# Loading v for batches two to four with casting transfers from GpSimd's queue

## The chip, the cores and the metric

The kernel runs on one core of a Trainium2 chip. The core has a TensorE (PE in the profile), a VectorE (DVE), a ScalarE (ACT), a GpSimd (POOL) and a SyncE (SP), each of which works through its own instructions in their order, and 16 DMA engines that they share. The time is the device time of one execution in microseconds; three runs of the kernel before gave 247.18, 247.3 and 246.52, median 247.18 us.

## What is computed

A retention layer feeds a Fourier mixing block with an MLP. There are 4 batches, 8 heads, 768 steps and 64 elements per head:

```python
for t in range(S):
    state = gamma[None, :, None, None] * state + np.einsum('bhd,bhe->bhde', k[:, :, t], v[:, :, t])
    y[:, :, t] = scale * np.einsum('bhd,bhde->bhe', q[:, :, t], state)

x = attn_out.transpose(0, 2, 1, 3).reshape(B, S, H * D)
mixed = np.real(np.fft.fft(np.fft.fft(x, axis=1), axis=2))
u = x + mixed
un = (u - mu) / np.sqrt(var + 1e-06)        # layer norm over the 512 features
out = u + np.maximum(un @ w_ch1, 0.0) @ w_ch2
```

The inputs q, k, v and the two weight matrices (512x2048 and 2048x512) are float32; the output is float32, 4 x 768 x 512.

## The kernel before

**Retention in chunks.** The 768 steps are cut into 6 chunks of 128, which lie on the 128 partitions, and heads are taken in pairs, so a batch has four steps of one head pair each. For a pair, q, k and v arrive as float32 tiles of 128 partitions x 768 elements. GpSimd makes 16-bit tiles of them: `q16`, `kd` (k times a decay per row) and `v16`. TensorE then forms the products of queries and keys inside each chunk (`a_unit`, line 600; VectorE masks them into `atm`, line 603), the state contribution of each chunk (`kv_unit`, line 619, a matmul of `kd` and `v16`; VectorE chains them into `s16`, line 629), and the output (`y_unit`: line 650 multiplies q by the states, line 654 multiplies `atm` by `v16`). In the first two batches TensorE transposes q and k (lines 439 and 556); in the last two the DMA engines do, in transfers that SP issues (lines 548 and 550).

**The mixing and the MLP.** The Fourier transforms are matmuls with tables (lines 736 and 833), with symmetric halves folded by VectorE (lines 679 to 705). GpSimd adds x to the result u (lines 870 and 872), VectorE takes the statistics, ScalarE subtracts the mean (line 891). The MLP runs in two halves of 384 rows per batch: `h_unit` (line 936, lines 953 for the first rows) and `ch_unit` (line 979), whose output VectorE scales and adds to u and SP stores (line 987).

**The order of the work.** Tiles come from pools of fixed size: 11 float32 input tiles for q, k and v, 4 for `v16`, 3 for `kd`. The first batch's retention is written out by hand in `first_units`, in a fixed order for every engine. Behind it, streams of units are merged by times of their own: the MLP of batch b, the retention of batch b + 1 (`attn_steps`) and its mixing. A step of `attn_steps` emits the casts of pair i (`cast_unit`), the state products of pair i - 1 (`kv_unit`) and the output of pair i - 2 (`y_unit`). A unit wrapped in `held` follows on each engine behind the instruction that was emitted last. A wait in front of an instruction therefore holds up everything that is behind it on its engine.

**The loads.** All of q, k and v are issued by SP at line 165, three transfers of 384 KB per pair, in runs of 256 bytes (q of the first two batches in runs of 1536 bytes). The loads of the second batch wait for the seventh of the eight weight transfers and for a matmul of the first batch's MLP; those of the third and fourth wait for a score matmul of the batch before. The eight weight transfers (lines 993 and 1000) are issued by GpSimd, since they turn float32 into 16-bit on the way; each reads 1 MB in runs of 2 KB and writes 512 KB.

**The cast of v.** In `cast_unit` the cast of v (line 388) is the last of a pair's casts on GpSimd, behind q (line 373, or 380) and the two halves of kd (line 383). It reads the float32 tile with the head outside the chunk and writes `v16` with the chunk outside the head:

```python
v16 = vp.tile([P, NCH, 2, D], f16, tag="v16", name="v16")
last_cast[b, i] = nc.gpsimd.tensor_scalar(
    out=v16, in0=v32.rearrange("p h c d -> p c h d"), scalar1=1.0, scalar2=1.0,
    op0=ALU.mult, op1=ALU.mult)
```

In the first batch `v0_unit` does this (line 423), for the last pair half on VectorE (line 427).

Of the kernel before, what the change touches and what calls it, by code (L numbers as in the profile page):

```python
# [12 lines left out]
ALU = mybir.AluOpType  # L13
f32 = mybir.dt.float32
f16 = mybir.dt.float16
# [3 lines left out]
P = 128  # L19
# [24 lines left out]
def kernel(  # L44
# [106 lines left out]
                nc.tensor.matmul(wps, wz[:, 0:P], wz, start=True, stop=True)  # L151
        return run

    in_of, a_of = {}, {}
    w_dma = []
    srcs = {"q": q, "k": k, "v": v}

    def load_unit(b, i, after=None):
        def run():
            h0 = 2 * PAIR_ORDER[i]  # L160
            for name, src in srcs.items():
                t = inp.tile([P, 2, NCH, D], f32, tag="in32", name=f"{name}32")
                rows = "h (p c) d -> p h c d" if b < NPE and name == "q" else \
                    "h (c p) d -> p h c d"
                dma = nc.sync.dma_start(t, src[b, h0:h0 + 2].rearrange(rows, p=P))  # L165
                if after is not None:
                    for x in (w_dma[after].ins, lb[0]["mm"].ins):
                        tc.add_manual_dep(dma.ins, x.name,
                                          mybir.DependencyInfo(mybir.DependencyClass.Sync,
                                                               mybir.DependencyReason.DATA),  # L170
                                          reason="loads in turn")
                if b > 1:
                    tc.add_manual_dep(dma.ins, a_of[b - 1, 1].ins.name,
                                      mybir.DependencyInfo(mybir.DependencyClass.Sync,
                                                           mybir.DependencyReason.DATA),
                                      reason="loads behind the transposes")
                in_of[name, b, i] = t
        return run

    for i in range(4):  # L180
        load_unit(0, i)()
# [174 lines left out]
    x_edges(0)()  # L356


    at, q16_of, kd_of, v16_of, last_cast = {}, {}, {}, {}, {}

    def cast_unit(b, i):
        def run():
            h0 = 2 * PAIR_ORDER[i]
            q32, k32, v32 = (in_of.pop((n, b, i)) for n in "qkv")
            kd = kp.tile([P, NCH, 2, D], f16, tag="kd16", name="kd16")
            v16 = vp.tile([P, NCH, 2, D], f16, tag="v16", name="v16")
            with ExitStack() as es:
                if b < NPE:
                    if (b, i - 1) in last_cast:
                        es.enter_context(tc.issue_after(last_cast[b, i - 1].ins))  # L370
                    q16 = qzs[i % 2].rearrange("p h c d -> p (h c d)")[
                        :, 0:NCH * P].rearrange("p (c h d) -> p c h d", c=NCH, h=2)
                    es.enter_context(tc.issue_after(nc.gpsimd.tensor_scalar(
                        out=q16, in0=q32.rearrange("p h c d -> p c h d"), scalar1=1.0,
                        scalar2=1.0, op0=ALU.mult, op1=ALU.mult).ins))
                else:
                    q16 = qzs[i % 2]
                    for h2 in range(2):
                        dst = q16[:, h2, :, D * h2:D * h2 + D]
                        nc.gpsimd.tensor_scalar(out=dst, in0=q32[:, h2], scalar1=1.0,  # L380
                                                scalar2=1.0, op0=ALU.mult, op1=ALU.mult)
                for h2 in range(2):
                    kc = nc.gpsimd.tensor_scalar(out=kd[:, :, h2, :], in0=k32[:, h2],  # L383
                                                 scalar1=gkd[:, h0 + h2:h0 + h2 + 1],
                                                 scalar2=1.0, op0=ALU.mult, op1=ALU.mult)
                    if b < NPE:
                        es.enter_context(tc.issue_after(kc.ins))
                last_cast[b, i] = nc.gpsimd.tensor_scalar(  # L388
                    out=v16, in0=v32.rearrange("p h c d -> p c h d"), scalar1=1.0, scalar2=1.0,
                    op0=ALU.mult, op1=ALU.mult)  # L390
            q16_of[b, i], kd_of[b, i], v16_of[b, i] = q16, kd, v16
        return run

    def q0_unit(i):
# [22 lines left out]

    def v0_unit(i):
        def run():
            v32 = in_of.pop(("v", 0, i)).rearrange("p h c d -> p c h d")  # L420
            v16 = v16_of[0, i] = vp.tile([P, NCH, 2, D], f16, tag="v16", name="v16")
            n = NCH if i < 3 else 3
            last_cast[0, i] = nc.gpsimd.tensor_scalar(
                out=v16[:, 0:n], in0=v32[:, 0:n], scalar1=1.0, scalar2=1.0, op0=ALU.mult,
                op1=ALU.mult)
            if n < NCH:
                nc.vector.tensor_copy(v16[:, n:], v32[:, n:])
        return run

    def t0_unit(i, part):  # L430
# [46 lines left out]
    def kv0_unit(i):  # L477
        def run():
            st = at[0, i]
            kd, v16 = kd_of[0, i], v16_of[0, i]  # L480
            wkf = st["wkf"] = ps_g.tile([P, D * (NCH - 1)], f32, tag="g", name="wkK",
                                        padded_shape=[P, DM])
            wk = wkf.rearrange("p (e c) -> p e c", c=NCH - 1)
            for c in range(NCH - 1):
                for h2 in range(2):
                    nc.tensor.matmul(wk[64 * h2:64 * h2 + 64, :, c], kd[:, c, h2, :],
                                     v16[:, c, h2, :], start=True, stop=True)
        return run

    def sc_unit(i):  # L490
# [10 lines left out]
    def yi_unit(i, h2):  # L501
        def run():
            st = at[0, i]
            first = i < 3
            if first:
                st["y", h2] = ps_y.tile([P, NCH, D], f32, tag="y", name="wkY",
                                        padded_shape=[P, 8, D])
            y, atm, v16 = st["y", h2], st["atm"], v16_of[0, i]
            for c in range(NCH):
                nc.tensor.matmul(y[:, c, :], atm[:, c, h2, :], v16[:, c, h2, :],  # L510
                                 start=first and c == 0, stop=not first and c == NCH - 1,
                                 skip_group_check=True)
        return run
# [95 lines left out]
    def kv_unit(b, i):  # L609
        def run():  # L610
            st = at[b, i]
            hp = PAIR_ORDER[i]
            kd, v16 = kd_of[b, i], v16_of[b, i]
            s16 = sp.tile([P, NCH - 1, P], f16, tag="s16", name="s16")
            st["s16"] = s16
            for c0, n in ((0, 3), (3, 2)):
                wk = ps_g.tile([P, 3, P], f32, tag="g", name="wkK", padded_shape=[P, 4, P])
                for c in range(c0, c0 + n):
                    nc.tensor.matmul(wk[:, c - c0, :], kd[:, c].rearrange("p a b -> p (a b)"),  # L619
                                     v16[:, c].rearrange("p a b -> p (a b)"),  # L620
                                     start=True, stop=True)
                for c in range(c0, c0 + n):
                    if c == 0:
                        if ON_ACT["kv"][min(b, 2)]:
                            nc.scalar.copy(s16[:, 0], wk[:, 0])  # L625
                        else:
                            nc.vector.tensor_copy(s16[:, 0], wk[:, 0])
                    else:
                        nc.vector.scalar_tensor_tensor(out=s16[:, c], in0=s16[:, c - 1],  # L629
                                                       scalar=gk2[:, hp:hp + 1],  # L630
                                                       in1=wk[:, c - c0],
                                                       op0=ALU.mult, op1=ALU.add)
        return run

    def y_unit(b, i):
        def run():
# [14 lines left out]
                                     start=(c == 1), stop=False, skip_group_check=True)  # L651
            for h2 in range(2):
                for c in range(NCH):
                    nc.tensor.matmul(yk[h2][:, c, :], atm[:, c, h2, :], v16[:, c, h2, :],  # L654
                                     start=False, stop=(c == NCH - 1), skip_group_check=True)
                h = 2 * hp + h2
                x = xts[b % 2]
# [379 lines left out]
    def first_units():  # L1037
        def a(i):
            un = [am_unit(i, 0), am_unit(i, 1)]
            return un  # L1040

        def e(i, *hh):
            return [ae_unit(i, half, h2) for half, h2 in hh]
# [4 lines left out]
        def x(i):  # L1048
# [23 lines left out]
               te_unit(3, 1), yx_unit(2), gk_unit(o[3]), x0_unit(2, 0), x0_unit(2, 1),  # L1072
               t_act(4, 0), t_act(4, 1), filler(2), v0_unit(3)]
        un += [w1_unit(g) for g in range(1, 4)] + [w2_unit(g) for g in range(4)]
        un += a(3) + e(3, (0, 0), (1, 0)) + [kv0_unit(3), filler(4), sc_unit(3), t_act(4, 2)]
        un += e(3, (0, 1), (1, 1))
        un += [yx_unit(3), yi_unit(3, 0), x0_unit(3, 0), filler(1), yi_unit(3, 1), x0_unit(3, 1),
# [104 lines left out]
```

## Time and profile before

| | value |
|---|---|
| runs | 247.18, 247.3, 246.52 us; median 247.18 us |
| span of the profiled execution, first to last instruction | 245.4 us |
| its own time beside the span | not on the page; the median of the runs is 1.78 us more than the span |
| TensorE busy | 234.2 us (95%) |
| VectorE, ScalarE, GpSimd busy | 177.0, 124.2, 81.7 us |
| DMA queue of SP | 94,960 packets, 31.86 MB, 62.2% of the 16 engines' span |
| DMA queue of GpSimd | 4,224 packets, 4.19 MB, 10.7% |
| loads of v from SP | 16 of 384 KB, median 6.3 us from issue to landing |
| casts of v on GpSimd, batches two to four | 12, 10.0 us in all, 831 ns each |

Bytes are counted as written. A busy share is an average over stages; which engine sets the pace has to be read stage by stage. A wait is given with what ended it, and idle time on an engine that others do not wait for costs nothing. The issuing of a DMA is not counted as busy time of its engine on the page, but stands in the timeline with a duration; the data lands later.

### The profile page before, as it was taken

The numbers are of one execution on the slowest core, as the hardware profiler recorded it, in microseconds if no ns is written. First come the engines' busy times: TensorE is split into PE (matmuls) and PEld (weight loads), VectorE is DVE, ScalarE is ACT, GpSimd is POOL, SyncE is SP. The second block draws the span as 40 slices with busy tenths as digits, with TensorE's granted clock in tenths as the row PEclk, the third lists the DMA queues.
The fourth block names the chain that finished last, engine by engine and source line by source line (L and its number), as shares of the span: only waits on it lengthen the run. The fifth ranks groups of instructions, "written<-read, shape, count | busy, mean of one in ns | idle before, by whom it ended". The sixth has DMA issues, their size and how long they took to land.

```text
span 245.4 us, 5309 instructions
## 1 busy us (share of the span) xinstructions
PE 234.2 (95%) x2024; PEld 143.8 (59%) x2024; DVE 177.0 (72%) x430; ACT 124.2 (51%) x276; POOL 81.7 (33%) x146
## 2 busy tenths in 40 slices
PE   6997899999999998999999999999999999999995
PEld 2454668956776655665567546655666455445543
DVE  8997957897897788996885748887895656424112
ACT  8798669587775434751247414742247317202500
POOL 6667601465600057690000646660002405000000
PEclk9999999999999999999999999999999999999999
DMA  8999999699999377999999667786200241221012
GB/s 173 256 260 140 204 195 205 164 245 230 291 229 222 75 168 165 191 181 137 256 272 214 116 141 203 129 120 139 87 1 0 45 151 21 47 85 43 0 45 85
DMA packets 99209, 36.39 MB, mean 148 GB/s; under 512 B 89840, under 2 KB 96240, under 8 KB 99184
## 3 DMA queue, kind: packets, MB, share of 16 engines
q1 hardware_dynamic: 94960, 31.86, 62.2%
q0 software_dynamic: 4224, 4.19, 10.7%
q8 instruction: 16, 0.26, 0.5%
q14 instruction: 9, 0.07, 0.1%
HBM read 27.26 MB, written 6.29 MB: 137 GB/s over the span
## 4 chain that ended last, share of the span: by engine, by line
PE 71%; DMA 7%; DVE 7%; POOL 4%; ACT 4%; SPq 3%; issue 1%; POOLq 0%; ACTq 0%; DVEq 0%
PE psc L979 30%; PE psh L936 25%; DMA k<-in_k_dram 5%; PE ps L736 3%; SPq L165 3%; PE wkA L600 3%; DMA q<-in_q_dram 2%; PE wkY L654 2%; PE pq L833 2%; PE wkY L650 1%; POOL u L870 1%; PE wkK L619 1%; ACT un L885 1%; DVE bst L889 1%; POOL kd L407 1%
## 5 line engine op out<-in xcount | busy, mean ns | idle before, releaser
L979 PE MATMUL psc<-w,ht 128*128 128x512 f16 (+2 forms) x400 | 89.3, 371 | 0.0
L936 PE MATMUL psh<-unT,w 128*128 128x384 f16 x448 | 81.6, 326 | 0.4 <-ACT ht L940 0.2
L979 PEld LDWEIGHTS <-ht 128*128 128x128 f16 x400 | 37.5, 98 | 36.5 <-issue 0.2
L936 PEld LDWEIGHTS <-w 128*128 128x128 f16 x448 | 42.3, 98 | 24.7 <-issue 1.4
L940 ACT ACTIVATE ht<-psh 128x384 f16<-128x384 f32 x64 | 30.9, 489 | 41.7 <-PE psh L936 41.1
L870 POOL TENSOR_TENSOR u<-u,x 128x256 f32<-128x256 f32 x21 | 13.3, 635 | 100.3 <-DVE u L840 91.0
L983 DVE SCALAR_TENSOR_TENSOR ob<-psc,stats,u 128x512 f32<-128x512 f32 (+2 forms) x25 | 18.1, 726 | 26.1 <-PE psc L979 26.0
L942 DVE TENSOR_SCALAR ht<-psh 128x384 f16<-128x384 f32 x48 | 26.2, 548 | 7.7 <-PE psh L936 7.4
L603 DVE TENSOR_TENSOR atm<-wkA,maskp 128x512 f16<-128x512 f32 x36 | 23.8, 681 | 1.6 <-PE wkA L600 1.6
L891 ACT ACTIVATE un<-u,stats 128x512 f16<-128x512 f32 x21 | 15.2, 722 | 16.7 <-DVE stats L890 12.1
L889 DVE BATCH_NORM_STATS2 bst<-u 128x6 f32<-128x512 f32 x21 | 14.6, 694 | 7.7 <-POOL u L872 7.6
L629 DVE SCALAR_TENSOR_TENSOR s<-s,gk,wkK 128x128 f16<-128x128 f16 x48 | 16.3, 341 | 3.7 <-ACT s L625 2.7
L662 ACT ACTIVATE x<-wkY,gexp 128x384 f16<-128x384 f32 x24 | 12.8, 581 | 8.0 <-PE wkY L654 8.0
L151 PE MATMUL wps<-ht 128*128 128x512 f16 x40 | 13.5, 444 | 2.2 <-POOL ht L202 2.2
L383 POOL TENSOR_SCALAR kd<-k,gexp 128x384 f16<-128x384 f32 x24 | 13.8, 585 | 3.6 <-DMA k<-in_k_dram 3.6
L872 POOL TENSOR_TENSOR u<-u,x 128x256 f32<-128x256 f32 x21 | 13.3, 635 | 3.0 <-DVE stats L890 3.0
L600 PE MATMUL wkA<-qTz,kT 128*128 128x256 f16 x72 | 13.4, 273 | 0.1
L835 ACT COPY qn<-pq 128x128 f32<-128x128 f32 x18 | 4.9, 272 | 13.6 <-PE pq L833 13.6
L953 PE MATMUL psh<-unT,w 128*128 128x128 f16 x192 | 11.5, 219 | 0.1
L953 PEld LDWEIGHTS <-w 128*128 128x128 f16 x192 | 11.0, 98 | 0.7 <-issue 0.5
L840 DVE SCALAR_TENSOR_TENSOR u<-pq,g,qn 128x256 f32<-128x256 f32 x18 | 8.5, 472 | 3.3 <-PE psh L936 2.5
L388 POOL TENSOR_SCALAR v<-v 128x768 f16<-128x768 f32 x12 | 10.0, 831 | 1.3 <-DMA v<-in_v_dram 1.3
(164 smaller groups left out, 315.6 us busy)
## 6 DMA issues: line engine op xcount, KB each, us to landing
q<-in_q_dram SPq DMA_DIRECT2D x16, 384.0 KB, 6.3
k<-in_k_dram SPq DMA_DIRECT2D x16, 384.0 KB, 5.6
v<-in_v_dram SPq DMA_DIRECT2D x16, 384.0 KB, 6.3
out_dram<-ob SPq DMA_DIRECT2D x23, 256.0 KB, 2.6
w<-in_moe_w_ch_dram POOLq DMA_DIRECT2D x8, 512.0 KB, 10.8
unT<-un SPq DMA_TRANSPOSE x15, 2.4
out_dram<-ob SPq DMA_DIRECT2D x1, 192.0 KB, 1.9
qTz<-q16z SPq DMA_TRANSPOSE x8, 3.9
```

The lines of the kernel that those rows point to most:

```text
L600: mm = nc.tensor.matmul(wk[:, c2], st["kT"][:, c, :], st["qT"][:, :, c, :], start=True, stop=True)
L603: nc.vector.tensor_tensor(out=st["atm"][:, 2 * part:2 * part + 2], in0=wk, in1=maskp[:, PAIR_ORDER[i]].unsqueeze(1).to_broadcast([P, 2, 2, ...
L629: nc.vector.scalar_tensor_tensor(out=s16[:, c], in0=s16[:, c - 1], scalar=gk2[:, hp:hp + 1], in1=wk[:, c - c0], op0=ALU.mult, op1=ALU.add)
L870: nc.gpsimd.tensor_tensor(out=u[:, kb, 0:256], in0=u[:, kb, 0:256], in1=x[:, kb, 0, 1:257], op=ALU.add)
L889: nc.vector.bn_stats(bst, u[:, kb, :])
L891: una = nc.scalar.activation(un, u[:, kb, :], AF.Identity, bias=stats[:, kb, 0:1], scale=-1.0)
L936: nc.tensor.matmul(psh, w116[:, cb, fb * P:(fb + 1) * P], unT[:, cb, rt * 384:(rt + 1) * 384], start=(cb == 0), stop=(cb == 3))
L940: nc.scalar.activation(ht16[:, fb, :], psh, AF.Relu, bias=0.0, scale=-1.0)
L942: nc.vector.tensor_scalar(out=ht16[:, fb, :], in0=psh, scalar1=-1.0, scalar2=0.0, op0=ALU.mult, op1=ALU.max)
L953: mm = nc.tensor.matmul(psh[:, f], w116[:, cb, fb * P:(fb + 1) * P], unT[:, cb, kb * P:(kb + 1) * P], start=(cb == 0), stop=(cb == 3))
L979: nc.tensor.matmul(psc[:, c0:c1], ht16[:, fb, rb3 * P:(rb3 + 1) * P], w216[:, fb, c0:c1], start=(fb == 0), stop=(fb == NFB - 1))
L983: nc.vector.scalar_tensor_tensor(out=ob[:, c0:c1], in0=psc[:, c0:c1], scalar=lb[b]["st"][:, rb, 3:4], in1=lb[b]["u"][:, rb, c0:c1], op0=AL ...
```

## The change

For the second, third and fourth batch, v is no longer loaded by SP and cast by GpSimd. One transfer per pair, issued by GpSimd, reads the float32 values and writes them as 16-bit values straight into `v16`. The tile now has the head outside the chunk, as the source has it, so the matmuls read it as `v16[:, h2, c, :]`, and `kv_unit` reads two runs of 64 elements instead of one of 128. The first transfer of a batch (pair 0) is issued a batch ahead: that of the second batch right behind the weights, those of the third and fourth behind the casts of the last pair of the batch before. The transfers of pairs 1 to 3 are issued behind the two kd casts of the pair before. The first batch's v is still loaded by SP and cast; only its tile has the new order. On SP 12 transfers are gone; on GpSimd 12 casts are gone and 12 transfers are added. On the other engines the order is the same, but for three matmuls of line 936 that move from in front of six transposes of kd (pair 3 of the second batch) to behind them.

```diff
@@ load_unit
             for name, src in srcs.items():
+                if b and name == "v":
+                    continue
                 t = inp.tile([P, 2, NCH, D], f32, tag="in32", name=f"{name}32")
...
+    def v_load(b, i):
+        h0 = 2 * PAIR_ORDER[i]
+        t = v16_of[b, i] = vp.tile([P, 2, NCH, D], f16, tag="v16", name="v16")
+        return nc.gpsimd.dma_start(t, v[b, h0:h0 + 2].rearrange("h (c p) d -> p h c d", p=P))
...
@@ cast_unit
-            q32, k32, v32 = (in_of.pop((n, b, i)) for n in "qkv")
+            q32, k32 = (in_of.pop((n, b, i)) for n in "qk")
...
                 for h2 in range(2):
-                    kc = nc.gpsimd.tensor_scalar(out=kd[:, :, h2, :], in0=k32[:, h2],
...
+                    last_cast[b, i] = nc.gpsimd.tensor_scalar(
+                        out=kd[:, :, h2, :], in0=k32[:, h2],
...
-                last_cast[b, i] = nc.gpsimd.tensor_scalar(
-                    out=v16, in0=v32.rearrange("p h c d -> p c h d"), scalar1=1.0, scalar2=1.0,
-                    op0=ALU.mult, op1=ALU.mult)
+                if i < 3:
+                    last_cast[b, i] = v_load(b, i + 1)
+                elif b + 1 < B:
+                    v_load(b + 1, 0)
...
@@ v0_unit
-            v32 = in_of.pop(("v", 0, i)).rearrange("p h c d -> p c h d")
-            v16 = v16_of[0, i] = vp.tile([P, NCH, 2, D], f16, tag="v16", name="v16")
+            v32 = in_of.pop(("v", 0, i))
+            v16 = v16_of[0, i] = vp.tile([P, 2, NCH, D], f16, tag="v16", name="v16")
...
@@ kv_unit
                     nc.tensor.matmul(wk[:, c - c0, :], kd[:, c].rearrange("p a b -> p (a b)"),
-                                     v16[:, c].rearrange("p a b -> p (a b)"),
+                                     v16[:, :, c, :],
...
@@ first_units
         un += [w1_unit(g) for g in range(1, 4)] + [w2_unit(g) for g in range(4)]
+        un += [lambda: v_load(1, 0)]
```

## The prediction

> **What bounds the kernel now.** I read the table of stretches first, since v is touched only from 45 us on (the first batch keeps its loads). Columns: stretch, length, then busy us of PE, PEld, DVE, ACT and POOL, granted clock, DMA share, GB/s.
>
> ```profile
> 50.00:55.00 5.00, 5.00 (x40) 2.88 (x39) 5.00 (x20) 4.29 (x8) 2.83 (x5) 1.00 1.22 248
> 55.00:60.00 5.00, 4.70 (x45) 3.04 (x44) 3.79 (x11) 3.93 (x7) 2.81 (x4) 1.00 1.18 249
> 60.00:65.00 5.00, 4.93 (x60) 3.27 (x58) 3.87 (x9) 3.70 (x6) 2.81 (x4) 1.00 1.14 235
> 100.00:110.00 10.00, 10.00 (x93) 6.81 (x92) 9.49 (x24) 6.39 (x16) 8.06 (x14) 1.00 1.08 173
> 150.00:165.00 15.00, 14.81 (x138) 9.27 (x135) 13.56 (x35) 8.89 (x22) 11.92 (x21) 1.00 0.81 152
> ```
>
> PE has no gaps to speak of where v is loaded and cast, at full clock (1.00). Over 45 to 242.48 us, where the last matmul ends, it is busy 195.63 of 197.48 us: 1.85 us idle. So a saving on POOL or SP can buy 1.85 us at most, and anything that makes PE wait is paid in full. Next, who ended PE's waits after 45 us:
>
> ```profile
> PE pst L920 <- ACT un L891: 0.7, 1, 0.7
> PE tq L556 <- POOL kd L383: 0.3, 1, 0.3
> ```
>
> Only the 0.3 us hangs on the loads. Third, POOL's timeline in the second batch, where each cast waits for its load:
>
> ```profile
> 50.28 1.15 POOL L383 TENSOR_SCALAR kd<-k,gexp 128x384 f16<-128x384 f32 x2 [0.26 <-DMA k<-in_k_dram]
> 51.85 0.83 POOL L388 TENSOR_SCALAR v<-v 128x768 f16<-128x768 f32 x1 [0.43 <-DMA v<-in_v_dram]
> 55.69 1.15 POOL L383 TENSOR_SCALAR kd<-k,gexp 128x384 f16<-128x384 f32 x2 [0.89 <-DMA k<-in_k_dram]
> 57.18 0.83 POOL L388 TENSOR_SCALAR v<-v 128x768 f16<-128x768 f32 x1 [0.34 <-DMA v<-in_v_dram]
> ```
>
> and PE's timeline, where a pair's v is first read:
>
> ```profile
> 55.83 0.44 PE L619 MATMUL wkK<-v,kd 128*128 128x128 f16 x5
> 59.63 0.44 PE L619 MATMUL wkK<-v,kd 128*128 128x128 f16 x5
> 64.71 0.44 PE L619 MATMUL wkK<-v,kd 128*128 128x128 f16 x5
> 69.55 0.44 PE L619 MATMUL wkK<-v,kd 128*128 128x128 f16 x5
> ```
>
> Last, what transfers cost: the page's issues (count, KB, us to landing), GpSimd's queue, and the issue of four weights on POOL.
>
> ```profile
> v<-in_v_dram SPq DMA_DIRECT2D x16, 384.0 KB, 6.3
> w<-in_moe_w_ch_dram POOLq DMA_DIRECT2D x8, 512.0 KB, 10.8
> q0 software_dynamic: 4224, 4.19, 10.7%
> 25.38 2.99 POOL L1000 DMA_DIRECT2D w<-in_moe_w_ch_dram  x4
> ```
>
> **The change part by part.**
>
> *Twelve casts off POOL.* 12 x 0.831 = 10.0 us, all beside a busy PE. POOL is 33% busy; its longest waits are for VectorE's u (91.0 us). Worth 0.
>
> *Twelve issues onto POOL.* A weight transfer (528 packets) took 0.75 to 0.96 us to issue; v has 12 runs on 128 partitions, 1,536 packets and 16 more. Bounds: 0.77 us if the price is per transfer, 3 x 0.77 = 2.3 us if per packet. Nothing separates the two; I take the middle, 1.5 us, so 0.7 us more than the cast. Behind an issue stand the next pair's q cast and the u additions of lines 870 and 872 (at 96.54, 100.73 and 153.69 us). They start at most 2.3 - 0.83 = 1.5 us later. Cover: they feed the second half of `h_unit`, which in that stage starts at 124.47 us, and kT of the last pair (transposed from 111.43, landing 3.1 us later) is read at 120.77 us. 0; without that cover 1.5 us at each of two places.
>
> *The first transfer.* Its issue shares a completion semaphore with the first weight transfer, which POOL must see landed: issued at 20.41, landing 5.6 to 9.8 us later, by 30.2 us at worst. POOL ends the weight issues at 28.37 and has nothing that can start before 37.80. Hidden by over 5 us. Its data goes behind the weights. They end near 43.5, and the DMA share is 0.62, 0.27, 0.17, 0.00 and 0.22 in the half microseconds from 43.5 to 46: room for the 2 us of this v. So the loads of pair 1 come 2 us earlier than before, and its kd cast too (near 53.6 instead of 55.69): PE's 0.3 us wait and 0.07 us at 61.98 go. Minus 0.4 us, the only gain in the sum (bounds 0 and 0.4).
>
> *Twelve loads off SP.* A v issue held SP 1.33 us (median). What is behind it, stores and transposes, mostly waits for VectorE (47.1 us) and POOL; PE waits for none of it. The 11 input tiles now hold more pairs, so the loads of k and v that SP issued as late as 97.16 and 102.64 us disappear or come earlier. 0.
>
> *The new deadline.* This decides. The transfer of pair i + 1 starts behind kd of pair i; PE reads it at line 619. From kd's end to that read, in the order of before: 8.2 us for pair 1 of the second batch (51.43 to 59.63), 7.9 and 7.6 for pairs 2 and 3 (about 10 with kd 2 us earlier); 9.55, 9.8, 9.2 in the third; 12.9, 9.2, 8.8 in the fourth. Price x = issue + landing. Landing: SP's loads span 3.2 to 7.8 us under load; the first four weights 5.6 to 9.8, each behind the last. I take 5.6, the least queued row on this queue, which covers twice the bytes and a third of the packets. x = 1.5 + 5.6 = 7.1 us (bounds 0.77 + 3.2 = 4.0 and 2.3 + 7.8 = 10.1). Spare: 1.1 us in the tightest place. 0.
>
> *Strided reads on PE.* 60 matmuls of line 619 read two runs of 64. Line 600 reads two runs of 128 at 0.22 us per two, full rate. 0; doubled it would be 60 x 56 ns = 3.3 us.
>
> *The first batch's new order.* The same number of elements; the q cast of line 398, one order permuted, took 0.83 us like line 388. 0. The three moved matmuls run on a full PE: 0.
>
> Sum: 245.4 - 0.4 = 245.0 us of span; with the 1.78 us that lie between span and median, **246.8 us**, call it no change. What a measurement of this kernel can tell from no change is 0.3%, 0.74 us.
>
> **The rivals.**
>
> *v comes late (slower).* Place: line 619 of pairs 1 to 3. A batch loses its largest x minus spare, since the next pairs shift along: x - 8.2, x - 9.2 and x - 8.8 us. It decides (over 0.74 + 0.4 us lost) from x = 9.1 us. At 9.5: 1.3 + 0.3 + 0.7 - 0.4 = +1.9, 249.1 us; at 10.1: +3.7, 250.9. For it: small packets. SP's loads of the third batch took 288 packets per engine in 6.2 us, 21.5 ns each; a weight packet 99.5 ns (10.7% of 245.4 us x 16 engines / 4,224). At 21.5 ns a v is 2.1 us of transfer, at 99.5 ns 9.6 us, and x at least 11. Against: the price follows bytes, 256 against 2,048. The Trainium skill, DMA: Bandwidth & Descriptors, section Specifications, says that writes under 512 bytes become read-modify-write, and the new runs are 128 bytes; no row of before has such writes. If by that a v took 4.2 us instead of 2.1 us, x would be 9.2, an estimate, and the end 248.2 us.
>
> *VectorE holds the issue (slower).* A kd cast took 1.27 us at 21.41 beside VectorE's fold at line 679, else 0.58: a factor of 2.2. On 1.5 us that makes 3.3, x = 8.9 and +0.4 us; on 2.3 it makes 5.1, x = 10.7 and +5.5. I put it at 249. Against: weight issues beside a VectorE busy 4.93 of 5 us took 0.77 to 0.80. The Trainium skill, SBUF — State Buffer, section SBUF: two separate sides, has this as a trap: GpSimd cannot write descriptors while VectorE runs in a two-port mode, 620 ns alone and 3,100 beside such an operation. By that estimate, x = 9.6 and +2.2 us; the rows here show at most 0.2.
>
> *PE's reads slow down (slower).* 3.3 us, 250.1; line 600 speaks against it.
>
> *The rest of PE's gaps close (faster).* If 10 us less reading by POOL let VectorE and ScalarE run ahead, up to 1.85 us go: 245.3; half of it 246.2. It takes 0.74 us to count; the 0.7 us at line 920 hangs on ScalarE and POOL's adds, which come before the casts.
>
> **How the numbers follow.** Hidden 0.42, v late 0.29, held issue 0.09, slow reads 0.06, gaps closed 0.14. Faster 0.14, within 0.3% 0.42, slower 0.44. The likeliest single case is 246.8, its own range 246.4 to 247.5. The range runs from 246.0 (half the gaps) to 251.2 (x at 10.1 us and a little more).
>
> **What would show it.** Right: 12 issues of v on POOL near 1.5 us, landing within 6 us; no wait of PE at line 619 for v; POOL's kd of pair 1 near 53.6 us; PE near 234 us busy. Wrong: PE idle for the DMA of v in front of line 619, first near 59.6 us; issues over 2.3 us; line 619 over 0.44 us per five.

## The result, and the profile after

The changed kernel takes 258.83 us (median of 256.16, 259.13, 259.35 and 258.53), the kernel before 246.97 us in the runs beside it: a ratio of 1.0454, with a 95% interval from 1.0403 to 1.0506. The change costs about 11.9 us where the forecast was no change, and the time lies outside the range given. The traced execution is the one of 256.16 us; its span is 254.3 us, 8.9 us more than before. Of that, 7.3 us are idle time of PE (18.5 us against 11.2, span less busy time), and 1.6 us are PE being busy longer (235.8 us against 234.2). The other three executions took 2.4 to 3.2 us more. Their mean granted clock was 0.980 to 0.987, against 0.993 in the traced one; 0.6 to 1.3% of 257 us would be 1.5 to 3.3 us, so a lower clock of PE can account for most of it. None of the three was traced, so at which places stays open. Of two kernels below (e2_third_fourth and e4_f32) the traced execution ran at a lower granted clock and is left out of their ratios; only which waits there are is read from it.

The table of stretches, after (columns as before: busy us of PE, PEld, DVE, ACT and POOL, granted clock, DMA share, GB/s):

```profile
50.00:55.00 5.00, 5.00 (x40) 2.86 (x39) 5.00 (x20) 4.29 (x8) 4.25 (x8) 1.00 1.23 278
55.00:60.00 5.00, 4.75 (x46) 3.01 (x45) 4.86 (x12) 3.98 (x7) 4.66 (x6) 1.00 1.51 250
100.00:110.00 10.00, 9.40 (x85) 6.45 (x86) 9.10 (x22) 6.00 (x15) 8.08 (x14) 1.00 1.22 155
150.00:165.00 15.00, 13.41 (x114) 8.59 (x115) 11.25 (x29) 8.03 (x22) 9.24 (x16) 1.00 0.79 135
165.00:180.00 15.00, 12.75 (x103) 6.90 (x101) 8.82 (x21) 2.66 (x8) 2.81 (x5) 0.89 0.92 116
```

The second batch (first two rows) is as full as it was. The idle time is in the third and fourth batch: 0.60 us in 100 to 110, where PE had no gap before, 1.59 us in 150 to 165 (0.19 before) and 2.25 us in 165 to 180. Who ended PE's waits from 45 us on:

```profile
PE wkA L608 <- DMA kT<-kd: 3.7, 3, 2.3
PE psh L944 <- DMA unT<-un: 2.6, 1, 2.6
PE pst L928 <- ACT un L899: 0.7, 1, 0.7
```

Two new lines stand above the one that was first before, 6.3 us together. Both are waits for tiles that the DMA engines transpose: kT (line 558, 550 before) for the products of queries and keys, and unT (line 924, 916 before) for the MLP. No wait for v is in the list. The issues, after (count, KB where the page gives them, median us from issue to landing), with GpSimd's queue:

```profile
v<-in_v_dram POOLq DMA_DIRECT2D x12, 192.0 KB, 6.9
unT<-un SPq DMA_TRANSPOSE x15, 2.4
kT<-kd SPq DMA_TRANSPOSE x8, 6.2
q0 software_dynamic: 22848, 6.55, 25.9%
```

and the row of kT before:

```profile
kT<-kd SPq DMA_TRANSPOSE x8, 3.1
```

The transposes of kT are issued by the same engine, from the same line and in the same form, and land after 6.2 us instead of 3.1. The median of unT did not move, but its longest went from 4.2 to 6.1 us. How they meet v is seen in the timelines of POOL, SP and PE of the changed kernel (start, duration, instruction, and the wait before it in brackets):

```profile
51.20 1.09 POOL L185 DMA_DIRECT2D v<-in_v_dram  x1
...
53.81 1.15 POOL L389 TENSOR_SCALAR kd<-k,gexp 128x384 f16<-128x384 f32 x2 [0.65 <-DMA k<-in_k_dram]
54.90 1.06 POOL L185 DMA_DIRECT2D v<-in_v_dram  x1
...
143.41 1.14 POOL L389 TENSOR_SCALAR kd<-k,gexp 128x384 f16<-128x384 f32 x2
144.50 1.08 POOL L185 DMA_DIRECT2D v<-in_v_dram  x1
```

```profile
143.96 1.43 SPq L556 DMA_TRANSPOSE qTz<-q16z  x1
145.48 1.57 SPq L924 DMA_TRANSPOSE unT<-un  x1
...
147.77 1.37 SPq L558 DMA_TRANSPOSE kT<-kd  x1
```

```profile
151.09 1.14 PE L944 MATMUL psh<-unT,w 128*128 128x384 f16 x6 [2.57 <-DMA unT<-un]
```

The changed kernel issues v directly behind the kd casts of a pair (51.20, 54.90 and 144.50 us are three of the places), and kd is what the transpose of kT waits for. So in the third and fourth batch v's issue falls among the transposes of qTz, unT and kT. At 144.50 us it falls between qTz and unT: unT is issued at 145.48 and lands 5.5 us later; before, it was issued at 143.99, landed after 2.7 us, and PE read it at 146.84 without a wait.

What the packets do in that moment is in the counts of packets by queue (q1 is SP's, q0 GpSimd's; packets, MB, share of 16 engines). Before, from 145 to 146 us and from 145.0 to 145.5 us:

```profile
q1 hardware_dynamic: 862, 0.21, 109.8%
...
q1 hardware_dynamic: 411, 0.10, 110.0%
```

After, from 147.4 to 147.9 us and from 148.8 to 149.3 us (shares that add up to more than 100% mean that the times of packets overlap on an engine):

```profile
q0 software_dynamic: 260, 0.03, 103.3%
...
q1 hardware_dynamic: 205, 0.05, 82.5%
q0 software_dynamic: 200, 0.03, 78.6%
```

Alone, the transposes move 411 packets of 256 bytes in half a microsecond. In the first stretch after, unT is issued and not landed, and only v's packets move. In the second, 205 transpose packets move beside 200 of v: one for one, and at half the rate. One packet of v takes 103.3% x 0.5 us x 16 / 260 = 31.8 ns, so a v of 1,536 packets is 1,536 x 31.8 / 16 = 3.05 us of every engine's time, which is about what kT's landing grew by (6.2 - 3.1 = 3.1 us). The Trainium skill, DMA: Bandwidth & Descriptors, section Queues, rings and completion order, says that an engine takes turns between the queues that have work, packet by packet, where its packet is typically a batch of some 9 to 17 descriptors. The 205 against 200 agree; the 260 against none, while unT was issued and not landed, do not look like turns, nor do the 367 of v against 96 from 148.0 to 148.5 us.

### The profile page after: what moved, and what is told of

It is laid out like the page before. It is cut to its first block, busy times and chain, and to the rows that moved or that the text cites. A ratio compares the mean times of both kernels' runs of the same rounds, so it can differ in the third digit from the quotient of the medians.

```text
span 254.3 us, 5291 instructions
## 1 busy us (share of the span) xinstructions
PE 235.8 (93%) x2024; PEld 143.9 (57%) x2024; DVE 178.9 (70%) x430; ACT 124.1 (49%) x276; POOL 84.3 (33%) x146
## 2 busy tenths in 40 slices
DMA packets 99209, 34.03 MB, mean 134 GB/s; under 512 B 89840, under 2 KB 96240, under 8 KB 99184
## 5 line engine op out<-in xcount | busy, mean ns | idle before, releaser
L987 PE MATMUL psc<-w,ht 128*128 128x512 f16 (+2 forms) x400 | 90.7, 374 | 0.0
L944 PEld LDWEIGHTS <-w 128*128 128x128 f16 x448 | 42.3, 98 | 27.5 <-issue 4.2
L151 PE MATMUL wps<-ht 128*128 128x512 f16 x40 | 12.8, 422 | 2.2 <-POOL ht L209 2.2
L608 PEld LDWEIGHTS <-kT 128*128 128x128 f16 x72 | 6.7, 101 | 11.4 <-DMA kT<-kd 5.3
L185 POOL DMA_DIRECT2D v<-in_v_dram x12 | 12.9, 1073 | 0.0
L633 ACT CAST s<-wkK 128x128 f16<-128x128 f32 x12 | 3.2, 267 | 18.6 <-issue 13.7
```

The costliest lines, as they stand in the source:

```text
L608: mm = nc.tensor.matmul(wk[:, c2], st["kT"][:, c, :], st["qT"][:, :, c, :], start=True, stop=True)
L944: nc.tensor.matmul(psh, w116[:, cb, fb * P:(fb + 1) * P], unT[:, cb, rt * 384:(rt + 1) * 384], start=(cb == 0), stop=(cb == 3))
L987: nc.tensor.matmul(psc[:, c0:c1], ht16[:, fb, rb3 * P:(rb3 + 1) * P], w216[:, fb, c0:c1], start=(fb == 0), stop=(fb == NFB - 1))
```

## Experiments

All are made from the changed kernel.

**Which batches.** e1_second keeps the casting transfers in the second batch alone, whose q and k TensorE transposes; e2_third_fourth keeps them in the third and fourth alone, whose q and k the DMA engines transpose. The rest is loaded by SP and cast by GpSimd, into the new tile order.

```diff
+VB = (1,)            # e2_third_fourth: (2, 3)
-                if b and name == "v":
+                if b in VB and name == "v":
...
+                if b not in VB:
+                    v16_of[b, i] = vp.tile([P, 2, NCH, D], f16, tag="v16", name="v16")
+                    last_cast[b, i] = nc.gpsimd.tensor_scalar(
+                        out=v16_of[b, i], in0=in_of.pop(("v", b, i)), scalar1=1.0, scalar2=1.0,
+                        op0=ALU.mult, op1=ALU.mult)
...
```

> Casting transfers for the second batch alone; the third and fourth batch load v from SP and cast on GpSimd as before (in the new tile order). Theory (the transfers of v take engine time from the DMA transposes of q, k and un, which run only in the third and fourth batch, and TensorE waits for these): as before, 246.3 to 247.7 us, kT landing after about 3.1 us. Rival (a casting transfer costs about 1 us wherever it is, by its issue, its landing or the new tile order): a third of the 12 us loss, about 251 us.

> Casting transfers for the third and fourth batch alone, the second as before. Theory (transposes delayed): the whole loss, 256 to 260 us, kT landing after about 6 us, TensorE waiting for kT and unT. Rival (a cost per transfer): two thirds of the loss, about 255 us, and the second batch contributes the rest.

e1_second took 247.15 us, ratio 1.0002 (0.9988 to 1.0016); e2_third_fourth took 258.05 us as the median of four, and its ratio of 1.0354 (1.0328 to 1.038) goes by the two executions at 255.83 and 255.93 us, just under the range that was expected. In the second batch the transfers cost nothing; in the third and fourth they cost 3.5%, beside 4.5% for the changed kernel. The two executions have a mean granted clock of 0.993, and so has the one of the changed kernel that took 256.16 us, so at equal clock the third and fourth batch carry the whole loss. The issues and then the waits of e2_third_fourth:

```profile
v<-in_v_dram POOLq DMA_DIRECT2D x8, 192.0 KB, 6.2
...
kT<-kd SPq DMA_TRANSPOSE x8, 5.9
```

```profile
PE wkA L614 <- DMA kT<-kd: 4.9, 2, 2.5
PE psh L950 <- DMA unT<-un: 2.7, 1, 2.7
```

They are the same two lines as in the changed kernel. In e1_second neither is in the list, and kT lands in 3.2 us.

**Away from the transposes.** e3_early keeps all twelve casting transfers, but issues the four of the third batch together behind the last score matmul of the second batch, and those of the fourth behind that of the third, when no transpose is under way. It has 8 tiles for v16 instead of 4 and 9 input tiles instead of 11.

```diff
-    inp = pool("inp", 11)
-    vp = pool("vp", 4)
+    inp = pool("inp", 9)
+    vp = pool("vp", 8)
...
-                if i < 3:
+                if b == 1 and i < 3:
                     last_cast[b, i] = v_load(b, i + 1)
-                elif b + 1 < B:
-                    v_load(b + 1, 0)
...
+    def v_early(b):
+        def run():
+            for i in range(4):
+                dma = v_load(b + 1, i)
+                tc.add_manual_dep(dma.ins, a_of[b, 3].ins.name, ...)
+        return run
...
```

> All twelve casting transfers stay; those of the third and fourth batch are issued together behind the last score matmul of the batch before (8 tiles for v16, 9 instead of 11 input tiles), when no transpose of that batch is in flight. Theory: kT lands after about 3 us again, no wait of TensorE for kT or unT, 246 to 247.5 us. Rival (issue on GpSimd, strided reads, cost per transfer): over 250 us.

e3_early took 247.12 us, ratio 1.0004 (0.9985 to 1.0023). The loss is gone with the same transfers, the same bytes and the same queue. Its issues:

```profile
v<-in_v_dram POOLq DMA_DIRECT2D x12, 192.0 KB, 8.0
...
kT<-kd SPq DMA_TRANSPOSE x8, 3.1
```

kT is back at 3.1 us, and v itself takes longer to land (8.0 us, four behind each other), which nobody waits for. It does not beat the kernel before either: what it takes off POOL and SP was not what PE waited for.

**The transfer alone, read by nobody.** In e3_early not only the collision has gone, v also arrives earlier. So e7_extra_full takes e3_early and puts back, at the changed kernel's places in the third and fourth batch, six transfers into spare tiles that nobody reads (two of them, with 6 tiles for v16 instead of 8); e8_extra_half makes each transfer one head instead of two.

```diff
+HEADS = 2            # e8_extra_half: 1
...
+                if b > 1 and i < 3:
+                    h1 = 2 * PAIR_ORDER[i + 1]
+                    t = scr.tile([P, HEADS, NCH, D], f16, tag="extra", name="extra")
+                    last_cast[b, i] = nc.gpsimd.dma_start(
+                        t, v[b, h1:h1 + HEADS].rearrange("h (c p) d -> p h c d", p=P))
...
```

> The kernel that issues all casting transfers of the third and fourth batch together behind the score matmuls of the batch before (e3_early, 247.12 us), plus six additional casting transfers that nobody reads: in the third and fourth batch, behind kd of pairs 0 to 2, v of the next pair goes once more into a spare tile, at the place where the changed kernel has it. Theory (what costs is the transfer beside the transpose of kT that the same kd starts, not that v is needed then): the loss comes back, kT lands in about 6 us, PE waits for kT, 254 to 260 us. Rival (what costs in the changed kernel is how v's arrival orders the work behind it): 246.5 to 249 us.

> As e7_extra_full, but the six additional transfers, read by nobody, bring one head instead of two: half the bytes and half the packets. Theory (the transpose is late by the packets that take turns with its own): kT lands in about 4.5 us, 249 to 255 us, between e3_early and e7_extra_full. Rival (a fixed cost of any transfer beside a transpose): the same as e7_extra_full within 1 us.

e7_extra_full took 258.28 us, ratio 1.0447 (1.0408 to 1.0485), close to the changed kernel's 1.0454. e8_extra_half took 251.66 us, ratio 1.0167 (1.0144 to 1.0191). Issues and then PE's waits of e7_extra_full:

```profile
extra<-in_v_dram POOLq DMA_DIRECT2D x6, 192.0 KB, 6.7
...
kT<-kd SPq DMA_TRANSPOSE x8, 5.8
```

```profile
PE wkA L613 <- DMA kT<-kd: 5.3, 3, 2.4
PE psh L949 <- DMA unT<-un: 3.1, 1, 3.1
```

and of e8_extra_half:

```profile
extra<-in_v_dram POOLq DMA_DIRECT2D x6, 96.0 KB, 4.9
...
kT<-kd SPq DMA_TRANSPOSE x8, 4.5
```

```profile
PE psh L949 <- DMA unT<-un: 1.7, 1, 1.7
PE wkA L613 <- DVE s L642: 1.3, 1, 1.3
PE wkA L613 <- DMA kT<-kd: 0.7, 1, 0.7
```

A transfer whose data nobody uses brings the whole loss back, so neither the deadline of v nor what is read from its tile has a part in it. The six issues on GpSimd come back too, at 1.08 us each, but the 5.8 us of kT are counted from kT's own issue on SP, so they are not what is late there. Half a transfer delays kT by 4.5 - 3.1 = 1.4 us, close to half of 3.05 us, and PE's waits for the two transposed tiles fall from 8.4 to 2.4 us. That is more than half, since each tile had some time to spare. The wait for VectorE in the list of e8_extra_half (0.9 us in e7_extra_full) was not followed further.

**Fewer packets.** e5_long_runs leaves the changed kernel as it is but reads v in runs of 1,536 bytes.

```diff
-        return nc.gpsimd.dma_start(t, v[b, h0:h0 + 2].rearrange("h (c p) d -> p h c d", p=P))
+        return nc.gpsimd.dma_start(t, v[b, h0:h0 + 2].rearrange("h (p c) d -> p h c d", p=P))
```

> The changed kernel with one alteration: v is read from memory in runs of 1,536 bytes (six rows of a head side by side in one partition), 256 runs in a transfer instead of 1,536. The rows of v land in another order than kT's and q's, so the sums pair the wrong rows; the work on every engine is the same. Theory (the transfer of v takes turns, packet by packet, with the packets of kT's transpose, so a v of fewer packets delays it less): kT lands in about 4.5 us instead of 6.2, PE waits less for kT and unT, 249 to 254 us. Rival (what costs is that any casting transfer runs beside a transpose, whatever its packets): kT stays near 6.2 us and the time at 256 to 260 us.

It took 251.58 us, ratio 1.0182 (1.0141 to 1.0222): within the theory's range, but kT lands in 5.5 us, not 4.5. Its issues:

```profile
v<-in_v_dram POOLq DMA_DIRECT2D x12, 192.0 KB, 5.5
...
kT<-kd SPq DMA_TRANSPOSE x8, 5.5
```

GpSimd's queue in 8 us in which one v is moved, in the changed kernel (144 to 152 us) and here (142 to 150 us), and here from 146 to 147 us, where SP's queue has no packet:

```profile
q0 software_dynamic: 1552, 0.20, 38.1%
...
q0 software_dynamic: 272, 0.20, 22.9%
...
q0 software_dynamic: 58, 0.04, 64.9%
```

With the same bytes, v takes 22.9% x 8 us = 1.83 us of every engine instead of 38.1% x 8 us = 3.05: a packet six times as large lasts 108 ns on average, not six times 31. So fewer packets make v shorter, and the loss falls from 11.6 to 4.3 us, as the theory had it. How late a transpose becomes is not settled by this: kT still lands 2.4 us later than beside no v, which is more than 1.83. From 146 to 147 us no transpose moved, although unT, issued at 144.07 us, landed only 5.0 us later, and v's 58 packets fill no more than 64.9% of the engines' time. What holds the transposes then, these runs don't show. The issue on POOL is 0.3 us shorter. Between the traced executions of the two kernels lie 4.9 us of span: 2.7 us are PE's waits for the two tiles (3.6 us instead of 6.3), and 2.0 us are PE's busy time (233.8 us instead of 235.8). The other 2.4 us between the medians lie in executions without a trace, of the changed kernel at a mean clock of 0.980 to 0.987, here at 0.993 to 1.000.

**The plain load.** e4_f32 leaves the transfers on GpSimd's queue and at their places, but lets them bring float32 into input tiles, and GpSimd cast.

```diff
-        t = v16_of[b, i] = vp.tile([P, 2, NCH, D], f16, tag="v16", name="v16")
+        t = in_of["v", b, i] = inp.tile([P, 2, NCH, D], f32, tag="in32", name="v32")
...
+                v16_of[b, i] = vp.tile([P, 2, NCH, D], f16, tag="v16", name="v16")
+                last_cast[b, i] = nc.gpsimd.tensor_scalar(
+                    out=v16_of[b, i], in0=in_of.pop(("v", b, i)), scalar1=1.0, scalar2=1.0,
+                    op0=ALU.mult, op1=ALU.mult)
```

> The transfers stay on GpSimd's queue and at their places, but bring float32 into an input tile (256-byte writes), and GpSimd casts as before. Theory (any second stream beside the transposes delays them): as the changed kernel, 255 to 261 us, kT landing after 5 us or more. Rival (the cast or its 128-byte writes make the stream dear): under 250 us, kT back near 3 us.

It took 269.43 us as the median of four; the ratio of 1.0889 (1.0857 to 1.0921) goes by the three from 268.45 to 269.79 us. That is outside both ranges. PE waits longest for the same tile:

```profile
PE wkA L612 <- DMA kT<-kd: 10.7, 4, 7.5
PE wkA L612 <- DVE s L641: 5.0, 1, 5.0
PE psh L948 <- DMA unT<-un: 3.0, 1, 3.0
```

This run is inconclusive on the cast. v shares the 11 input tiles with q and k again, so loads of q and k that had to wait for a tile stand between the transposes in SP's queue (at 97.03, 100.91, 108.56 and 109.23 us), and that alone can make kT late. Nor are the packets those of the changed kernel: GpSimd's queue has 5,568 packets and 8.91 MB, against 4,224 and 4.19 MB before, so about 3.5 KB in each packet of v and not the 256 bytes that were expected.

**The tile order.** e6_layout has no casting transfer at all: loads and casts as before, and only v16 in the new order, with the matmuls that read it in two runs.

```diff
+VB = ()
-                if b and name == "v":
+                if b in VB and name == "v":
...
```

> No casting transfer at all: loads by SP and casts by GpSimd as before, in all batches, only the new order of the v tile (head, chunk, dim) with the matmuls that read it in two runs of 64. Theory (the order costs nothing): 246.5 to 247.7 us, five matmuls of the line that multiplies kd with v at 0.44 us. Rival (strided reads on TensorE cost): 249 to 250 us, those five matmuls above 0.44 us.

It took 247.33 us, ratio 0.9998 (0.9987 to 1.0008). A matmul of kd and v takes what it took:

```profile
L633 PE MATMUL wkK<-v,kd 128*128 128x128 f16 x60 | 5.3, 219 | 0.0
```

## Why the prediction was wrong

**The step that failed is "Twelve loads off SP".** It looked at what stands behind v's issue on SP's queue, found "stores and transposes", and put both at 0 because "PE waits for none of it". PE did not wait for the transposes before because each landed ahead of its first read, some of them barely, and no part of the prediction asked what the moved transfer would do to them on the engines that they share. "Twelve issues onto POOL" even used kT's 3.1 us as cover, unchanged, and for the one place with much room: the last pair of the third batch, read at 120.77 us. (The 3.1 us are a median; that kT landed after 4.1.) In place of nothing, the runs showed kT landing 3.1 us later and PE waiting 6.3 us for kT and unT.

The cost could have been worked out from the trace of before. Two of the tightest places in it are unT in the fourth batch and kT of its pair 2 (issue on SP, first read on PE):

```profile
143.99 1.51 SPq L916 DMA_TRANSPOSE unT<-un  x1
146.84 1.46 PE L936 MATMUL psh<-unT,w 128*128 128x384 f16 x8
...
160.52 1.54 SPq L550 DMA_TRANSPOSE kT<-kd  x1
165.67 0.38 PE L600 MATMUL wkA<-qTz,kT 128*128 128x256 f16 x2
```

Between landing and first read of kT were, in the third batch, 99.81 - (94.92 + 3.0) = 1.9 us for pair 0 and 113.15 - (108.38 + 3.1) = 1.7 for pair 2, in the fourth 165.67 - (160.52 + 4.4) = 0.75 for pair 2, and for unT 146.84 - (143.99 + 2.7) = 0.15; the other pairs of these batches had 2.4 us or more. Had v been charged to them with 3.05 us, these four would have lost 1.15, 1.35, 2.3 and 2.9 us, 7.7 in all. Measured were waits of 0.91, 0.56, 2.25 and 2.57 us, 6.3 in all. Even by the 2.1 us that the prediction gave for v's transfer, unT (1.95) and kT of pair 2 of the fourth batch (1.35) come to over 3 us, enough to forecast slower. The trace of before even has such a meeting in small: the unT issued at 103.31 us, next behind the load of v at 102.64, landed after 4.2 us, against a median of 2.4; in e3_early, where that load is gone, the same unT (at 102.18) landed after 2.5.

**"The new deadline" looked at the right transfer from the wrong side.** Its price x came out as 1.08 + 6.9 = 8.0 us against 7.1, close to the tightest spare of 8.2, and still v was late for nobody: there is no wait for v in front of line 627 (619 before), and the transfers of e7_extra_full, which nobody reads, cost the same. The transfer itself was mis-sized, at 21.5 ns a packet (2.1 us); a packet of v took 31.8 ns (3.05 us), between that and the 4.2 us of its estimate for small writes. That "no row of before has such writes" holds for 128 bytes only: of the 99,209 packets of before, 89,840 were under 512 bytes, those of SP's loads at 21.5 ns among them.

**The rivals on the slower side** named other mechanisms. v late: fell, as said. VectorE holding the issue: fell; each issue took 1.06 to 1.09 us in the second batch, beside a VectorE busy 5.00 of 5 us. PE's reads slow: fell with e6_layout and with this row of the changed kernel, line 627 from 55 to 70 us (duration in ns, minimum, median, maximum):

```profile
L627 PE MATMUL wkK<-v,kd x20: 219/219/219, 55.8 to 69.5; 128*128 128x128 f16 x20
```

So the chance of slower (0.44) rested on reasons other than the one that made the kernel slower, and its largest time, 251.2 us, fell short by 7.6 us.

**What held.** *The first transfer*: POOL's timeline above shows kd of pair 1 of the second batch at 53.81 us, forecast near 53.6. In e1_second, PE's idle time from 45 to 90 us is 0.25 us where it was 0.60 before: 0.35 us of the 0.4 forecast. In its median (247.15 beside 247.22) that can't be told from no change. *Twelve casts off POOL* at 0: e3_early has all casts of batches two to four off POOL and is no faster, so the gaps of PE do not close. *Twelve issues onto POOL* at 0 holds for POOL itself, at 1.08 us each where 1.5 was taken, and *Strided reads on PE* and *the first batch's new order* at 0 hold by e6_layout.

**PE's clock** is a small part of the traced execution. In the stretch of the longest wait for kT (165 to 180 us) the granted clock is 0.89; PE's busy time grew by 1.6 us in all. No step had it.

## What to carry to other kernels

A transfer that is moved has to be charged to whatever else the DMA engines do at that moment, and not only against its own deadline: list the transposes and loads started by the same event, take from each the time between its landing and its first read, and subtract the engine time of the newcomer (packets x time of one / 16). Here that is an estimate: it came near the delay of kT in the changed kernel (3.05 against 3.1 us), and was too small in e5_long_runs (1.83 against 2.4). A wait that is missing from the profile says nothing about how much slack there is: here 0.15 to 1.9 us were left at four places, and a 3 us transfer ran through all of them. If a transfer is not urgent, it can be issued where nothing that PE soon needs is in flight; that brought the 4.5% back (e3_early).

## What the hardware showed that was not expected

- A DMA transpose beside a casting transfer on another queue lands later: kT after 3.1 us alone, 4.5 us beside 96 KB (as written), 5.8 to 6.2 us beside 192 KB, and 5.5 us beside 192 KB read in long runs.
- The time that a casting transfer takes of the engines goes neither with its bytes nor with its packets alone: 192 KB took 3.05 us of every engine in packets of 128 bytes (31 ns each) and 1.83 us in packets of 768 bytes (108 ns each).
- The issue on GpSimd has a large fixed part. 256 runs took 0.77 us (e5_long_runs), 768 took 0.89 us (e8_extra_half), 1,536 took 1.08 us: about 0.23 to 0.25 ns more for each run, on some 0.7 us.
- The granted clock of PE fell after one pause and not after another. After the wait of 2.25 us that ended at 172.66 us it was 0.65 (172.5 to 175 us), and two matmuls of line 608, at 174.22 us, took 0.63 us instead of 0.38. After the wait of 2.57 us that ended at 151.09 us it stayed at 1.00 (151 to 156 us). What decides it, these runs don't show.
